# Attention with a mixture of experts on one core: the transition's masks, first gathers, first expert products and last gate weights in another order

## Chip, cores and metric

One Trainium2 chip, 1 core. The metric is the device time of one execution, in microseconds (us).

## What is computed

8 batches of 8 heads of causal attention (576 positions, head size 64, a bias from a running sum, softmax) give 4608 rows of 512 numbers. Each row goes to one of 16 experts and comes back times its gate weight:

```python
scores = scale * np.matmul(q, k.transpose(0, 1, 3, 2))
scores = np.where(causal, -1000000000.0, scores + np.minimum(bias, 0.0))
attn = np.exp(scores - np.max(scores, axis=-1, keepdims=True))
attn_out = np.matmul(attn / (np.sum(attn, axis=-1, keepdims=True) + 1e-09), v)
x = attn_out.transpose(0, 2, 1, 3).reshape(B * S, H * D)
g_idx = np.argmax(x @ w_group, axis=1)            # 4 groups
# within a group: e_idx = argmax(x @ w_expert[g]), 4 experts each
h = np.maximum(x[mine] @ w1[g, e], 0.0)           # 512 -> 1024
out[mine] = (g_w * e_w)[mine][:, None] * (h @ w2[g, e])
```

## The kernel before

**Attention and routing.** The heads run through a pipeline: row maxima (PE, DVE), scores (PE), exp from PSUM into the tiles pt and pu (ACT, L274), zeros above the diagonal by an affine select on POOL (`mask`, L283), then the product with the values (PE, L304), copied out by ACT. Pairs of heads are normalised and transposed into xT (DVE), rounded to xTh (ACT, L362) with the remainder xTl (L366), and turned back into rows that a DMA stores to the DRAM tensor xs. `Router.batch` follows a batch behind: logits, their transposes plt (L789), a chain on DVE from the maximum to the one-hot `hot` (L797 to L818), counts per expert by PE products into pc (L825), then on DVE the place of each row (L842 to L858), its selector tiles col, rows and val (L862 to L873), and products `listed` (L880) that write the row numbers (pi) and the gate weights (pw) of each expert's list. The weights come from Exp (L897) and a chain of twelve small operations (L904 to L922), which ACT writes back as c3p (L923); val 2 to 4 (L931) wait for it, and pw for them.

**Experts.** Each of 16 slots takes one expert's rows by indirect DMA from xs (`gather`, L599, on POOL's queue), transposes them on PE (px, L1058), splits each into a rounded part (xh, ACT, L1059) and the remainder (xl, DVE, L1060), and multiplies: eight groups ph (L1108) with the rounded weights wh and both parts, then with the low weights wl and xh; a group's relu is split again into hh (ACT, L1103) and hl (DVE, L1104); then four groups py of w2 (L1163). Rounded weights are cast by ACT (L1007), the low ones made by POOL (L1010) or DVE (L1016). The first slot takes 256 rows of an expert that is chosen behind batch 6, so that it can start before the last batch is routed; `start()` does that: it reduces the lists to ids, issues two gathers and picks the next expert. The last batch's rows of that expert make one more tile of 128, `rest` (its transposed rows prr, split in xhr and xlr, L1237 to L1240; products pur, L1250). Slot 1 has 368 rows.

**What sets the order.** PE's order in the transition is that of the program text, inside `manual_schedule(engines={ENG.PE})` (L1337 on), where `run` calls lists of items one by one. The orders of DVE, ACT and POOL there come from a scheduler of the framework. `after(tc, i)` holds back what is issued until i is issued; `behind(tc, later, earlier)` orders two instructions of one engine without a semaphore. A key chain on DVE (L1305 to L1317: key, rank, sel, esl, esi) ranks the experts for the later slots.

Of the kernel before, what the change touches and what calls it, by code (L numbers as in the profile page):

```python
# [8 lines left out]
F32 = mybir.dt.float32  # L9
# [45 lines left out]
def attn_moe(ctx, tc, qk, v, s, wr, w1, w2, out, stop_at=None, dbg=None):  # L55
# [24 lines left out]
    st.listed = {}  # L80

# [29 lines left out]
def attention(tc, qk, v, s, wr, xs, st):  # L111
# [3 lines left out]
    with ExitStack() as ctx:  # L115
# [138 lines left out]
        def scores(n, pt):  # L254
# [23 lines left out]
            def causal(u):  # L278
# [4 lines left out]
                nc.gpsimd.affine_select(out=d, in_=d, pattern=[[0, len(u)], [1, rows]], compare_op=ALU.is_ge, fill=0.0,  # L283
                                        base=0, channel_multiplier=-1)
# [3 lines left out]
        def av(n, pt, vals, sums):  # L288
# [4 lines left out]
            for half, todo in enumerate(avs):  # L293
# [4 lines left out]
                def item(j, t, qa, qb, half=half, base=base, w=w, po=po, last=len(todo) - 1):  # L298
                    if j == 0:
# [4 lines left out]
                    nc.tensor.matmul(po[0][:, qa - base:qb - base],  # L304
                                     VT[p % NVT].rearrange("p t a d -> p (t a d)")[:, (3 * t + 1 + h) * 64:][:, 0:P],
                                     x[:, c:c + qb - qa], start=(j == 0), stop=(j == last))
                    if j == last:
# [13 lines left out]
        def normalise(p, vals, sums):  # L321
# [312 lines left out]
class Router:  # L634
# [106 lines left out]
    def start(self):  # L741
# [3 lines left out]
        first_ids(nc, sm, st, 0, 2, ((0, 0, 2, st.ids0[:, 0:2]),))  # L745
        for t in range(2):
            st.gathered = gather(nc, self.xs, st.xg0, P, t, st.ids0[:, t:t + 1], NTOK - S)
        yield
        self.pick(1)
        t = sm.tile([P, E], F32, name="ku")  # L750
        V.tensor_scalar(out=t, in0=st.count, scalar1=-1.0, scalar2=256.0, op0=ALU.mult, op1=ALU.add)
        V.scalar_tensor_tensor(out=t, in0=t, scalar=0.0, in1=st.first[:, 0], op0=ALU.max, op1=ALU.mult)
        V.tensor_tensor(out=st.count, in0=st.count, in1=t, op=ALU.add)
        yield

    def batch(self, b, xtail, xh, xl):
# [857 lines left out]
```

## Time and profile before

| | |
|---|---|
| median of 3 runs | 928.27 us (927.01 to 928.57) |
| the profiled execution's own time | 927.77 us |
| its span, first to last instruction | 926.1 us |
| mean granted clock of TensorE | 0.987 |
| busy: PE, DVE, ACT, POOL | 93, 76, 68, 71% |

Attention takes up about 0 to 445 us of the span, the experts about 445 to 912. A busy share is an average over both. A wait is idle time of an engine with the instruction that released it; the granted clock is a share of full speed, in a stretch or over the whole.

### The profile page before, as it was taken

What the parts mean: (1) busy time and instruction counts of PE and PEld (TensorE: products, weight loads), DVE (VectorE), ACT (ScalarE), POOL (GpSimd) and SP (SyncE); (2) the same over time, 40 slices, a digit from 0 to 9 for tenths busy, and PEclk for the clock granted to TensorE, in tenths of its full rate; (3) what the DMA queues carried; (4) which work ended last, traced back from release to release, by engine and by line L of the source; (5) the groups of instructions that cost most, each with busy time, mean ns of one, the idle gap of its engine ahead of it and who ended that gap; (6) DMA issues with size and microseconds to landing.
All of it is one profiled execution on the core that took longest, in us unless ns stands there. A gap on an engine that the chain in (4) does not pass through costs nothing. (4 is left out here: it accounts for less than half of the span.)

```text
span 926.1 us, 17738 instructions
## 1 busy us (share of the span) xinstructions
PE 864.9 (93%) x5649; PEld 780.6 (84%) x5649; DVE 701.4 (76%) x1989; ACT 629.5 (68%) x1373; POOL 660.1 (71%) x762
## 2 busy tenths in 40 slices
PE   4899999999999999998879999999999999999993
PEld 3788787888878787887778999899999999999992
DVE  7676686858778686866476788899888889888830
ACT  3688787888878787876736666666676666776640
POOL 8798686877868686844678656666678778877750
PEclk9999999999999999999989999999999999999997
DMA  7766655565646665323537545446555555665510
GB/s 150 182 165 164 147 143 145 144 157 140 155 107 159 147 156 134 101 84 138 188 128 225 182 173 184 166 163 218 193 203 183 192 185 207 229 218 194 181 44 23
DMA packets 65005, 148.10 MB, mean 160 GB/s; under 512 B 7588, under 2 KB 40996, under 8 KB 54728
## 3 DMA queue, kind: packets, MB, share of 16 engines
q1 hardware_dynamic: 55020, 126.98, 46.6%
q0 software_dynamic: 7488, 18.89, 5.7%
q10 hardware_dynamic: 2396, 1.02, 0.4%
q8 instruction: 47, 0.77, 0.4%
q14 instruction: 54, 0.44, 0.2%
HBM read 108.97 MB, written 19.69 MB: 139 GB/s over the span
## 5 line engine op out<-in xcount | busy, mean ns | idle before, releaser
L1010 POOL TENSOR_TENSOR wl<-raw,wh 128x512 fp32r<-128x512 f32 x182 | 232.9, 1302 | 59.7 <-ACT wh L1007 41.7
L158 POOL TENSOR_TENSOR WB<-r,WA 64x576 fp32r<-64x576 f32 x128 | 181.3, 1416 | 23.5 <-PE pm L207 10.9
L215 DVE CUSTOM_DVE_ANT_0 mx<-pm,mask 128x192 bf16<-128x192 f32 (+4 forms) x320 | 129.1, 419 | 39.1 <-PE pm L207 34.4
L1007 ACT CAST wh<-raw 128x512 fp32r<-128x512 f32 x256 | 153.9, 616 | 1.0 <-POOL wl L1010 0.7
L1108 PE MATMUL ph<-xl,wh 128*128 128x256 f32 (+13 forms) x512 | 146.8, 306 | 4.5 <-DVE xl L1080 4.5
L1108 PE MATMUL ph<-xh,wh 128*128 128x256 f32 (+13 forms) x512 | 145.5, 302 | 3.9 <-DVE xl L1060 2.7
L264 PE MATMUL ps<-WA 68*128 68x320 f32 (+4 forms) x384 | 136.6, 359 | 6.8 <-ACT pu L274 3.6
L207 PE MATMUL pm<-WA 66*128 66x288 f32 (+4 forms) x384 | 124.9, 353 | 17.4 <-DMA WA<-ch 9.8
L304 PE MATMUL po<-pt,VT 128*128 128x256 f32 (+3 forms) x512 | 122.1, 355 | 2.5 <-POOL pt L283 2.5
L1163 PE MATMUL py<-hl,wh 128*128 128x256 f32 (+13 forms) x448 | 113.4, 302 | 1.3 <-DVE hl L1104 1.3
L1163 PE MATMUL py<-hh,wh 128*128 128x256 f32 (+13 forms) x448 | 112.8, 301 | 0.0
L266 PE MATMUL ps<-WB 128*128 128x320 f32 (+4 forms) x384 | 110.6, 301 | 0.0
L1209 DVE STREAM_TRANSPOSE yr<-yT 32x384 f32<-32x384 f32 (+1 forms) x208 | 104.5, 502 | 4.3
L304 PE MATMUL po<-pu,VT 128*128 128x320 f32 (+1 forms) x384 | 105.2, 381 | 0.0
L1075 DVE STREAM_TRANSPOSE xt<-xg 32x256 f32<-32x256 f32 (+1 forms) x208 | 102.5, 493 | 3.2
L1108 PEld LDWEIGHTS ph<-xl,wh 128*128 128x128 f32 x512 | 97.8, 191 | 7.9 <-DVE xl L1080 6.4
L1108 PEld LDWEIGHTS ph<-xh,wh 128*128 128x128 f32 x512 | 97.8, 191 | 5.9 <-DVE xl L1060 3.0
L304 PEld LDWEIGHTS po<-pt,VT 128*128 128x128 f32 x512 | 87.4, 192 | 14.7 <-POOL pt L283 3.0
L1103 ACT ACTIVATE hh<-ph 128x256 fp32r<-128x256 f32 (+13 forms) x128 | 53.5, 420 | 62.3 <-PE ph L1108 61.9
L207 PEld LDWEIGHTS pm<-WA 66*128 66x128 f32 (+1 forms) x384 | 68.5, 190 | 30.6 <-DVE mc L215 13.1
L283 POOL TENSOR_SCALAR_AFFINE_SELECT pt<-pt 128x128 f32<-128x128 f32 (+2 forms) x192 | 63.7, 341 | 42.0 <-ACT pt L274 37.1
L1104 DVE SCALAR_TENSOR_TENSOR hl<-ph,hh 128x256 fp32r<-128x256 f32 (+13 forms) x128 | 59.3, 464 | 41.1 <-ACT hh L1103 39.2
(225 smaller groups left out, 1948.8 us busy)
## 6 DMA issues: line engine op xcount, KB each, us to landing
raw<-in_w_dram SPq DMA_DIRECT2D x64, 1024.0 KB
WB<-WA SPq DMA_DIRECT2D x64, 288.0 KB
r<-in_qk_dram SPq DMA_DIRECT2D x31, 576.0 KB
VT<-in_v_dram SPq DMA_DIRECT2D x32, 384.0 KB
xs<-xr SPq DMA_DIRECT2D x15, 512.0 KB
xs<-xrt SPq DMA_DIRECT2D x7, 128.0 KB
xg<-xs,ids POOLq DMA_INDIRECT x46, 4.5
out_dram<-yr,ids POOLq DMA_INDIRECT x43, 3.2
```

The lines of the kernel that those rows point to most:

```text
L158: i = nc.gpsimd.tensor_tensor(out=wb[64 * a:64 * a + 64, a, h], in0=r[:, h, a], in1=w[0:64, a, h, QO:].bitcast(F32), op=ALU.subtract)
L207: nc.tensor.matmul(ps[:rows, :cw], WA[i][0:66, QA, h, QO + q0:QO + q0 + rows], WA[i][0:66, KA, h, QO + c0:QO + c0 + cw], start=True, stop= ...
L215: nc.vector.tensor_tensor_reduce(out=tmp[:rows, :cw], in0=ps[:rows, :cw], in1=mk[:rows], scale=1.0, scalar=-3.0e38 if c0 == 0 else mo, op0 ...
L264: nc.tensor.matmul(ps[:rows, o:o + w], WA[i][0:68, KA, h, QO + k0:QO + k0 + rows], WA[i][0:68, QA, h, QO + q0:QO + q0 + w], start=True, st ...
L266: nc.tensor.matmul(ps[:rows, o:o + w], WB[p % NBB][:, KA, h, k0:k0 + rows], WB[p % NBB][:, QA, h, q0:q0 + w], start=False, stop=True)
L304: nc.tensor.matmul(po[0][:, qa - base:qb - base], VT[p % NVT].rearrange("p t a d -> p (t a d)")[:, (3 * t + 1 + h) * 64:][:, 0:P], x[:, c: ...
L1007: self.casts.append(nc.scalar.copy(h[:, j], raw[:, j]))
L1010: self.low = nc.gpsimd.tensor_tensor(out=l[:, j], in0=raw[:, j], in1=h[:, j].bitcast(F32), op=ALU.subtract)
L1075: V.transpose(dst[:, 0:n, :, j], src[:, 0:n, :, i])
L1108: self.product = nc.tensor.matmul(pss[f][:, :cap], w[f // 4][:, c, (f % 4) * P:(f % 4 + 1) * P], x[:, c, :cap], start=(c == 0 and w is sel ...
L1163: self.product = nc.tensor.matmul(pss[c][:, :cap], w[2 + f // 4][:, f % 4, c * P:(c + 1) * P], x[:, f, :cap], start=(f == 0 and w is self. ...
L1209: V.transpose(dst[:, 0:n, :, i], src[:, 0:n, :, j])
```

## The change

Four things, and the bookkeeping for them (lists st.masks, st.av, st.lows, st.counted, st.valued and products, to which instructions are appended as they are issued):

- `start()` yields twice more before the gathers and once between them; the second gather is ordered behind the third mask from the end, and a low part of xT (st.lows[-3]) behind the last mask. The choice of the next expert comes after the ids are written.
- The first slot's groups 0 to 3 are opened together on column blocks 0 and 1, then on 2 and 3; the transposes of its gathered rows are ordered ahead of the fourth attention product from the end; the first weight cast is ordered behind the xh of the last transposes, as `split` then names it, and the third behind the last sums of attention. The last batch's counts stand ahead of product 84 (the low products of group 5).
- `weights()` is the old code from Exp to c3p as a function. For the last batch it runs ahead of pi, with a PSUM tile of its own (pk) in place of room in pi's, and is no longer held behind the first ids.
- pi stands behind 40 products of py, pw behind all the first 24 low ones; the key chain comes after val 4, not after the first ids.

```diff
@@ -742,15 +745,18 @@
 
         nc, sm, st = self.tc.nc, self.sm, self.st
         V = nc.vector
-        first_ids(nc, sm, st, 0, 2, ((0, 0, 2, st.ids0[:, 0:2]),))
+        chosen = first_ids(nc, sm, st, 0, 2, ((0, 0, 2, st.ids0[:, 0:2]),))
+        yield
+        yield
         for t in range(2):
-            st.gathered = gather(nc, self.xs, st.xg0, P, t, st.ids0[:, t:t + 1], NTOK - S)
-        yield
-        self.pick(1)
-        t = sm.tile([P, E], F32, name="ku")
-        V.tensor_scalar(out=t, in0=st.count, scalar1=-1.0, scalar2=256.0, op0=ALU.mult, op1=ALU.add)
-        V.scalar_tensor_tensor(out=t, in0=t, scalar=0.0, in1=st.first[:, 0], op0=ALU.max, op1=ALU.mult)
-        V.tensor_tensor(out=st.count, in0=st.count, in1=t, op=ALU.add)
+            st.gathered.append(gather(nc, self.xs, st.xg0, P, t, st.ids0[:, t:t + 1], NTOK - S))
+            yield
+        with after(self.tc, chosen):
+            self.pick(1)
+            t = sm.tile([P, E], F32, name="ku")
+            V.tensor_scalar(out=t, in0=st.count, scalar1=-1.0, scalar2=256.0, op0=ALU.mult, op1=ALU.add)
+            V.scalar_tensor_tensor(out=t, in0=t, scalar=0.0, in1=st.first[:, 0], op0=ALU.max, op1=ALU.mult)
+            V.tensor_tensor(out=st.count, in0=st.count, in1=t, op=ALU.add)
         yield
 
     def batch(self, b, xtail, xh, xl):
...
@@ -886,41 +892,44 @@
                 V.tensor_tensor(out=dst, in0=dst, in1=ps[:, 0:(j1 - j0) * EL], op=ALU.add)
             return ps
 
-        yield 2
-        pi = listed(0, 2, "pi")
-        if b == B - 1:
-            st.routed = first_ids(nc, sm, st, 0, 3, ((0, 2, 3, st.ids0[:, 2:3]), (1, 0, 3, st.ids1)))
-        if b == B - 2:
-            for _ in self.start():
-                yield
-
-        nc.scalar.activation(ex, df, AF.Exp)
-        yield 1
-        wf = pi[:, 128:128 + NB * 5]
-        w = wf.rearrange("p (t g) -> p t g", g=5)
-        cwp, rem = pi[:, 160:160 + NB], pi[:, 168:168 + NB]
-        c3p = pi[:, 176:176 + 3 * NB].rearrange("p (j t) -> p j t", t=NB)
-        with after(tc, st.routed):
+        def weights(bank):
+            nc.scalar.activation(ex, df, AF.Exp)
+            yield 1
+            wf = bank[:, 128:128 + NB * 5]
+            w = wf.rearrange("p (t g) -> p t g", g=5)
+            cwp, rem = bank[:, 160:160 + NB], bank[:, 168:168 + NB]
+            c3p = bank[:, 176:176 + 3 * NB].rearrange("p (j t) -> p j t", t=NB)
             V.tensor_reduce(out=wf, in_=ex, axis=AX.X, op=ALU.add)
             V.tensor_scalar(out=wf, in0=wf, scalar1=1e-9, scalar2=None, op0=ALU.add)
             V.reciprocal(wf, wf)
-        yield
-        with after(tc, st.routed):
+            yield
             ws = T("ws", [NB, 4])
             V.tensor_tensor(out=ws, in0=w[:, :, 1:5], in1=oh[:, :, 0], op=ALU.mult)
             wsum = T("wsum", [NB])
             V.tensor_reduce(out=wsum, in_=ws, axis=AX.X, op=ALU.add)
             for x in (cwp, st.cw[:, b]):
                 V.tensor_tensor(out=x, in0=wsum, in1=w[:, :, 0], op=ALU.mult)
-        yield
-        with after(tc, st.routed):
+            yield
 
             c3 = T("c3", [3, NB], BF16)
             V.tensor_copy(c3[:, 0], cwp)
             V.tensor_tensor(out=rem, in0=cwp, in1=c3[:, 0], op=ALU.subtract)
             V.tensor_copy(c3[:, 1], rem)
             V.tensor_tensor(out=c3[:, 2], in0=rem, in1=c3[:, 1], op=ALU.subtract)
-        nc.scalar.copy(c3p, c3)
+            nc.scalar.copy(c3p, c3)
+            return c3, c3p
+
+        yield 2
+        if b == B - 1:
+            c3, c3p = yield from weights(self.ps_s(f"pk{b}"))
+        pi = listed(0, 2, "pi")
+        if b == B - 1:
+            st.routed = first_ids(nc, sm, st, 0, 3, ((0, 2, 3, st.ids0[:, 2:3]), (1, 0, 3, st.ids1)))
+        else:
+            if b == B - 2:
+                for _ in self.start():
+                    yield
+            c3, c3p = yield from weights(pi)
         for j in range(3):
             yield
             with after(tc, st.routed):
...
@@ -928,7 +937,8 @@
                     nc.gpsimd.tensor_tensor(out=val[:, 2 + j], in0=colf, in1=c3[:, j].unsqueeze(2).to_broadcast(C4),
                                             op=ALU.mult)
                 else:
-                    V.tensor_tensor(out=val[:, 2 + j], in0=colf, in1=c3p[:, j].unsqueeze(2).to_broadcast(C4), op=ALU.mult)
+                    st.valued = V.tensor_tensor(out=val[:, 2 + j], in0=colf,
+                                                in1=c3p[:, j].unsqueeze(2).to_broadcast(C4), op=ALU.mult)
         yield 2
         if b == B - 2:
             yield
...
@@ -1092,9 +1104,20 @@
                 def first(f):
 
                     pss[f] = acc(f"ph{u}_{f}")
-                    for c in range(4):
+                    half(f, 0)
+                    half(f, 2)
+
+                def half(f, c0):
+                    for c in (c0, c0 + 1):
                         for x in (self.xh, self.xl):
                             product(f, self.w.h, x, c)
+
+                def opening():
+                    for f in range(4):
+                        pss[f] = acc(f"ph{u}_{f}")
+                    for c in (0, 2):
+                        for f in (0, 3, 1, 2):
+                            half(f, c)
 
                 def last(f):
                     for c in range(4):
...
@@ -1114,8 +1137,8 @@
 
                 if u == 0:
 
-                    return [lambda f=f, part=part: part(f) for h in (0, 4) for part in (first, last)
-                            for f in range(h, h + 4)]
+                    return [opening] + [lambda f=f, part=part: part(f) for part, h in ((last, 0), (first, 4), (last, 4))
+                                        for f in range(h, h + 4)]
                 return [lambda f=f: item(f) for f in range(8)]
 
             def y_rows(self):
...
@@ -1285,7 +1308,10 @@
         cws = mc.tile([P, E, NL], F32, name="cws")
         wts = [Expert(0, st.e0[0:1, 0:1]), Expert(1, st.e0[0:1, 1:2])]
         first = Slot(0, wts[0], 256, xgs[0], st.ids0[:, 0:2], cws[:, 0])
-        first.last = st.gathered
+        first.last = st.gathered[1]
+        for i, k in ((1, 3),):
+            behind(tc, st.gathered[i], st.masks[-k])
+        behind(tc, st.lows[-3], st.masks[-1])
         rest = Tile("r", wts[0], xgs[0], st.ids0[:, 2:3], cws[:, 0, 2:3])
         run(wts[0].load((st.evacs[-3], st.xh, st.xrt, st.xrt), (first.last,) * 4, nc.gpsimd))
         rest.gather()
...
@@ -1296,7 +1322,7 @@
         with after(tc, slots[1].last, rest.last):
             nc.gpsimd.memset(yT[:, :, 2 * P:], 0.0)
 
-        order = after(tc, st.routed)
+        order = after(tc, st.valued)
 
         S3 = [P, E, E]
         ie, key, t3 = st.ie, st.key, st.t3
...
@@ -1336,15 +1362,20 @@
 
         with tc.manual_schedule(engines={ENG.PE}):
             run(X)
+            behind(tc, st.av[-4], first.turned)
+            behind(tc, wts[0].casts[0], first.split[0])
+            behind(tc, wts[0].casts[2], st.evacs[-1])
             h = first.h_items()
-            run(h[:12])
-            behind(tc, st.listed[0], first.product)
-            run(h[12:])
+            run(h)
+            made = first.products
+            behind(tc, made[84], st.counted)
             Y, R = first.y_items(), rest.items()
-            run(Y[:4])
-
-            behind(tc, st.listed[2], first.product)
-            run(Y[4:6] + R[:1])
+            del made[:]
+            run(Y[:6])
+            behind(tc, st.listed[0], made[39])
+            behind(tc, made[40], st.listed[0])
+            behind(tc, st.listed[2], made[-1])
+            run(Y[6:7] + R[:1])
             with after(tc, rest.split[1]):
                 by_slot(idf, idl, 0, E)
                 listed = V.tensor_copy(ids, idf)
...
@@ -1354,7 +1385,7 @@
                 V.tensor_tensor(out=cwl, in0=part[3], in1=part[4], op=ALU.add)
                 V.tensor_tensor(out=cwl, in0=cwl, in1=part[2], op=ALU.add)
                 by_slot(cws, cwl, 0, 1)
-            run(Y[6:] + R[1:5])
+            run(Y[7:] + R[1:5])
             W = wts[1].load((first.rounded, rest.split[0], None, None), (None, rest.split[1], None, None))
             run(W[:8])
             low = wts[1].low
```

On **POOL**, at the end of attention (pt and pu are the tiles of exp, two of each for two heads; xg the gathered rows). Before:

```order
L283 AFFINE_SELECT pu_118<-pu_118 128x128
L283 AFFINE_SELECT pt_117<-pt_117 64x64
L599 DMA xg_74<-xs,ids_69 128x512 x2
L283 AFFINE_SELECT pt_117<-pt_117 128x2x128
L928 TENSOR_TENSOR val_6109<-col_6093,c_6209 128x320
L283 AFFINE_SELECT pt_119<-pt_119 64x64
L283 AFFINE_SELECT pt_119<-pt_119 128x128
L283 AFFINE_SELECT pu_120<-pu_120 128x128
L283 AFFINE_SELECT pt_119<-pt_119 128x2x128
L366 TENSOR_TENSOR xTl_6036<-xT_6180,xTh_6035 128x512
```

With the change:

```order
L284 AFFINE_SELECT pu_118<-pu_118 128x128
L284 AFFINE_SELECT pt_117<-pt_117 128x2x128
L284 AFFINE_SELECT pt_117<-pt_117 64x64
L602 DMA xg_74<-xs,ids_69 128x512
L284 AFFINE_SELECT pt_119<-pt_119 64x64
L284 AFFINE_SELECT pt_119<-pt_119 128x128
L602 DMA xg_74<-xs,ids_69 128x512
L937 TENSOR_TENSOR val_6109<-col_6093,c_6228 128x320
L284 AFFINE_SELECT pu_120<-pu_120 128x128
L284 AFFINE_SELECT pt_119<-pt_119 128x2x128
L369 TENSOR_TENSOR xTl_6036<-xT_6162,xTh_6035 128x512
```

Both masks of the first head have moved in front of the first gather, two of the second head's between the gathers, and val behind both gathers.

On **DVE**, from the last batch's one-hot and counts to the lists (hl the remainder of a group of the first slot). Before:

```order
L818 TENSOR_TENSOR hot<-oh_6347,plt_6333 128x80
L1104 SCALAR_TENSOR_TENSOR hl_6593<-ph_4_6654,hh_6592 128x256
L842 TENSOR_TENSOR pc_6351<-pc_6351,count 128x80
L1104 SCALAR_TENSOR_TENSOR hl_6593<-ph_5_6663,hh_6592 128x256
L1104 SCALAR_TENSOR_TENSOR hl_6593<-ph_6_6672,hh_6592 128x256
L844 TENSOR_TENSOR off_6364<-pc_6351,hot 128x80
L845 TENSOR_TENSOR count<-count,pc_6351 128x16
L1104 SCALAR_TENSOR_TENSOR hl_6593<-ph_7_6681,hh_6592 128x256
L849 TENSOR_REDUCE pos<-off_6364 128x5
L849 TENSOR_REDUCE pc_6351<-off_6364 128x5
L854 TENSOR_TENSOR u_6369<-pc_6351,thr 128x20
L856 TENSOR_REDUCE pc_6351<-u_6369 128x5
```

With the change, a piece from the middle of the same stretch, behind the place chain that is interleaved with the gate weights:

```order
L915 CAST c_6392<-pk_6381 128x5
L868 TENSOR_TENSOR col_6374<-hot,pc_6351 128x320
L873 TENSOR_TENSOR rows_6376<-cols,pc_6351 128x640
L916 TENSOR_TENSOR pk_6381<-pk_6381,c_6392 128x5
L1127 SCALAR_TENSOR_TENSOR hl_6594<-ph_5_6664,hh_6593 128x256
L1127 SCALAR_TENSOR_TENSOR hl_6594<-ph_6_6673,hh_6593 128x256
L879 TENSOR_TENSOR val_6378<-col_6374,part 128x320 x2
L1127 SCALAR_TENSOR_TENSOR hl_6594<-ph_7_6682,hh_6593 128x256
L917 CAST c_6392<-pk_6381 128x5
L918 TENSOR_TENSOR c_6392<-pk_6381,c_6392 128x5
L892 TENSOR_TENSOR lists<-lists,pi_6398 128x128
```

hl of groups 5 to 7 stood right behind pc; now 5 and 6 stand behind rows, 7 behind val, and the gate weights' chain (c, pk) ends in front of the lists.

On **DVE**, around the second lists (xts and idl are made from the lists for all slots, wl is a weight of slot 1). Before:

```order
L1315 TENSOR_REDUCE esl<-t_73 128x16
L922 TENSOR_TENSOR c_6411<-pi_6381,c_6411 128x5
L1317 CAST esi<-esl 128x16
L931 TENSOR_TENSOR val_6378<-col_6374,pi_6381 128x320 x3
L886 TENSOR_TENSOR lists<-lists,pw_6420 128x192
L615 TENSOR_SCALAR xts<-idl 128x64
L616 SCALAR_TENSOR_TENSOR idl<-idl,xts 128x64
L1016 TENSOR_TENSOR wl_0_6874<-raw_0_6872,pw_0_0_6886 128x512
L1240 TENSOR_TENSOR xlr<-prr_x,xhr 128x4x128
L1329 TENSOR_TENSOR xts<-sel,idl 128x1024
L1016 TENSOR_TENSOR wl_1_6877<-raw_1_6875,pw_1_0_6897 128x512
```

With the change:

```order
L1337 TENSOR_TENSOR sel<-rank,ie 128x256
L892 TENSOR_TENSOR lists<-lists,pw_6421 128x192
L618 TENSOR_SCALAR xts<-idl 128x64
L1340 TENSOR_TENSOR t_73<-sel,ie 128x256
L619 SCALAR_TENSOR_TENSOR idl<-idl,xts 128x64
L1341 TENSOR_REDUCE esl<-t_73 128x16
L1343 CAST esi<-esl 128x16
L1026 TENSOR_TENSOR wl_0_6875<-raw_0_6873,pw_0_0_6887 128x512
L1263 TENSOR_TENSOR xlr<-prr_x,xhr 128x4x128
L1355 TENSOR_TENSOR xts<-sel,idl 128x1024
L1026 TENSOR_TENSOR wl_1_6878<-raw_1_6876,pw_1_0_6898 128x512
```

The val rows have left this place, and t, esl and esi of the key chain now stand between the lists and xlr.

## Rows read from the trace of the kernel before

**Rows 1.** The page, busy time by engine: us, share of the span, instructions.

```profile
...
PE 864.9 (93%) x5649; PEld 780.6 (84%) x5649; DVE 701.4 (76%) x1989; ACT 629.5 (68%) x1373; POOL 660.1 (71%) x762
```

**Rows 2.** Waits of PE, 425 to 500 us: line that waited, what released it, us in total, times, longest.

```profile
...
PE pw L880 <- DVE val L931: 5.1, 1, 5.1
PE ph L1108 <- DVE xl L1060: 2.7, 1, 2.7
PE po L304 <- POOL pt L283: 2.1, 1, 2.1
```

**Rows 3.** The same, 500 to 926 us.

```profile
...
PE ph L1108 <- DVE xl L1080: 4.5, 9, 1.0
```

**Rows 4.** Stretches of 2 us: length, PE busy (instructions), granted clock, DMA share, GB/s.

```profile
...
434.00:436.00 2.00, 1.30 (x3) 0.67 0.70 215
436.00:438.00 2.00, 2.00 (x9) 0.50 0.05 21
...
480.00:482.00 2.00, 1.11 (x6) 0.50 0.67 178
482.00:484.00 2.00, 2.00 (x10) 0.50 0.11 41
484.00:486.00 2.00, 2.00 (x12) 0.53 0.00 0
```

**Rows 5.** Timeline of PE: start, us, line, operation, out<-in, count [idle before <-releaser].

```profile
...
434.70 1.43 PE L304 MATMUL po<-pt,VT 128*128 128x320 f32 x2 [2.08 <-POOL pt L283]
...
439.48 0.27 PE L1058 MATMUL px<-ident,xg 128*128 128x128 f32 x1
...
447.61 0.39 PE L1108 MATMUL ph<-xh,wh 128*128 128x256 f32 x1 [2.73 <-DVE xl L1060]
...
453.03 0.76 PE L1108 MATMUL ph<-xh,wl 128*128 128x256 f32 x5
...
462.82 2.08 PE L1108 MATMUL ph<-xh,wl 128*128 128x256 f32 x16
464.74 0.32 PE L825 MATMUL pc<-hot,ub 128*128 128x64 bf16 x2
...
472.94 0.56 PE L880 MATMUL pi<-val,rows 128*128 128x128 bf16 x5
...
480.89 1.09 PE L880 MATMUL pw<-val,rows 128*128 128x192 bf16 x5 [5.05 <-DVE val L931]
```

**Rows 6.** Timeline of POOL, the same columns.

```profile
...
431.65 1.26 POOL L599 DMA_INDIRECT xg<-xs,ids  x1 [0.94 <-DVE c L919]
433.21 1.00 POOL L599 DMA_INDIRECT xg<-xs,ids  x1 [0.31 <-issue]
434.23 0.41 POOL L283 TENSOR_SCALAR_AFFINE_SELECT pt<-pt 128x256 f32<-128x256 f32 x1
...
480.46 0.54 POOL L1297 MEMSET yT<- 128x512 f32 x1
480.95 3.75 POOL L1010 TENSOR_TENSOR wl<-raw,wh 128x512 fp32r<-128x512 f32 x3
485.28 4.78 POOL L1010 TENSOR_TENSOR wl<-raw,wh 128x512 fp32r<-128x512 f32 x3 [0.58 <-ACT wh L1007]
```

**Rows 7.** Timeline of ACT.

```profile
...
428.52 0.60 ACT L274 ACTIVATE pt<-ps 128x512 f32<-128x512 f32 x1
...
479.35 0.17 ACT L923 CAST pi<-c 128x15 f32<-128x15 bf16 x1 [14.03 <-DVE c L922]
```

**Rows 8.** DMA issues, 430 to 440 us: count, KB each, median us from issue to landing.

```profile
...
xg<-xs,ids POOLq DMA_INDIRECT x2, 3.7
```

**Rows 9.** Timeline of DVE, from the last batch's logits to the end of its gate weights.

```profile
...
460.92 0.26 DVE L797 TENSOR_REDUCE lmx<-plt 128x25 f32<-128x100 f32 x1 [1.36 <-PE plt L789]
...
462.80 0.24 DVE L818 TENSOR_TENSOR hot<-oh,plt 128x80 bf16<-128x80 f32 x1
...
465.50 0.25 DVE L842 TENSOR_TENSOR pc<-pc,count 128x80 f32<-128x80 f32 x1 [0.59 <-PE pc L825]
...
466.55 0.42 DVE L1104 SCALAR_TENSOR_TENSOR hl<-ph,hh 128x256 fp32r<-128x256 f32 x1
...
468.55 0.81 DVE L867 TENSOR_TENSOR rows<-cols,pc 128x640 bf16<-128x640 f32 x1
469.28 1.65 DVE L873 TENSOR_TENSOR val<-col,part 128x320 bf16<-128x320 bf16 x2
...
475.63 0.26 DVE L904 TENSOR_REDUCE pi<-df 128x25 f32<-128x100 f32 x1
...
479.22 0.17 DVE L1317 CAST esi<-esl 128x16 int32<-128x16 f32 x1
```

**Rows 10.** Timeline of DVE, the lists and what follows.

```profile
...
474.13 0.19 DVE L615 TENSOR_SCALAR kemp<-kids 128x48 f32<-128x48 f32 x1
...
482.02 0.35 DVE L886 TENSOR_TENSOR lists<-lists,pw 128x192 f32<-128x192 f32 x1 [1.19 <-PE pw L880]
482.30 2.47 DVE L615 TENSOR_SCALAR xts<-idl 128x64 f32<-128x64 f32 x1
...
485.58 0.68 DVE L1240 TENSOR_TENSOR xlr<-prr_x,xhr 128x512 fp32r<-128x512 f32 x1
486.18 1.48 DVE L1329 TENSOR_TENSOR xts<-sel,idl 128x1024 f32<-128x1024 bf16 x1
```

More of the change, by code (lines that the diff above doesn't have):

```diff
@@ L80, in attn_moe @@
     st.listed = {}
+    st.masks, st.av, st.gathered, st.lows = [], [], [], []
     attention(tc, qk, v, s, wr, xs, st)
@@ L282, in causal @@
                 d = probs(pt, t, off)[:rows, 0:len(u) * w].rearrange("p (t q) -> p t q", q=w)[:, :, 0:rows]
-                nc.gpsimd.affine_select(out=d, in_=d, pattern=[[0, len(u)], [1, rows]], compare_op=ALU.is_ge, fill=0.0,
-                                        base=0, channel_multiplier=-1)
+                st.masks.append(nc.gpsimd.affine_select(out=d, in_=d, pattern=[[0, len(u)], [1, rows]],
+                                                        compare_op=ALU.is_ge, fill=0.0, base=0, channel_multiplier=-1))
             return [lambda u=u: item(u) for u in units]
@@ L303, in item @@
                             (pt[0], PC[t]))
-                    nc.tensor.matmul(po[0][:, qa - base:qb - base],
+                    i = nc.tensor.matmul(po[0][:, qa - base:qb - base],
                                      VT[p % NVT].rearrange("p t a d -> p (t a d)")[:, (3 * t + 1 + h) * 64:][:, 0:P],
                                      x[:, c:c + qb - qa], start=(j == 0), stop=(j == last))
+                    if n == NH - 1 and half:
+                        st.av.append(i)
                     if j == last:
@@ L824, in count @@
         def count(lhs, t0, t1, col, rows=P, start=False, stop=False):
-            nc.tensor.matmul(pc[:, col:col + (t1 - t0) * E], lhs[:rows],
-                             ohb[:rows, t0:t1].rearrange("p t e -> p (t e)"), start=start, stop=stop)
+            st.counted = nc.tensor.matmul(
+                             pc[:, col:col + (t1 - t0) * E], lhs[:rows], ohb[:rows, t0:t1].rearrange("p t e -> p (t e)"), start=start, stop=stop)
         count(self.ub, 0, 4, 0, start=True)
@@ L1043, in __init__ @@
                 self.rows = [min(P, cap - t) for t in range(0, cap, P)]
+                self.products = []
             def gather(self):
@@ L1107, in product @@
                 def product(f, w, x, c):
-                    self.product = nc.tensor.matmul(pss[f][:, :cap], w[f // 4][:, c, (f % 4) * P:(f % 4 + 1) * P], x[:, c, :cap],
-                                     start=(c == 0 and w is self.w.h and x is self.xh), stop=(c == 3 and w is self.w.l))
+                    self.products.append(nc.tensor.matmul(pss[f][:, :cap], w[f // 4][:, c, (f % 4) * P:(f % 4 + 1) * P], x[:, c, :cap],
+                                     start=(c == 0 and w is self.w.h and x is self.xh), stop=(c == 3 and w is self.w.l)))
                 def item(f):
@@ L1162, in product @@
                 def product(c, w, x, f, stop=None):
-                    self.product = nc.tensor.matmul(pss[c][:, :cap], w[2 + f // 4][:, f % 4, c * P:(c + 1) * P], x[:, f, :cap],
+                    self.products.append(nc.tensor.matmul(pss[c][:, :cap], w[2 + f // 4][:, f % 4, c * P:(c + 1) * P], x[:, f, :cap],
                                      start=(f == 0 and w is self.w.h and x is self.hh),
-                                     stop=(f == 7 and w is self.w.l) if stop is None else stop)
+                                     stop=(f == 7 and w is self.w.l) if stop is None else stop))
                 def item(c):
```

7 lines of the change are left out of this document (4 added, 3 removed).

## Prediction

> **What bounds the kernel now.** I read the page first, then the table of waits of TensorE for the transition and for what follows, then granted clock and busy time in short stretches, then the timelines of the four engines around each wait. The page says that PE is busy for 93% of the span [rows 1]: only time in which PE stands, or runs at its lower level, can be won. The transition from attention to the experts (about 425 to 500 us) holds 9.9 us of waits in three places: an attention product that waits for the causal mask (2.1), the first expert product that waits for the split of its gathered rows (2.7), and the last list product that waits for the gate weights (5.1) [rows 2]. In the 426 us behind it the largest sum of waits is 4.5 us for xl, in nine pieces [rows 3], so that what the transition gains should arrive at the end. The reader is to see in the stretches that each long wait has a second cost: behind the first and the last the granted clock is 0.50 to 0.67 while PE is fully busy, the lower of the two levels, 1.2 and not 2.4 GHz [rows 4]. In PE's timeline the same shows behind the second: 32 products take 5.42 us (447.61 to 453.03), whereas 16 with the same columns take 1.92 (462.82 to 464.74), 0.12 each [rows 5]. All is summed against the profiled execution, 927.77 us, 0.50 below the median of the runs shown.
>
> **What the change removes.**
>
> 1. *The mask.* Its input is ready at 429.12 (428.52 + 0.60) [rows 7], but POOL holds two gathers in front of it and masks at 434.23 [rows 6]. Now both masks of that head stand before the first gather. The wait goes, 2.08 [rows 5], and the half clock behind it: 1.30 us busy and 2.00 us busy, all at half, lose 0.65 + 1.00 = 1.65 [rows 4]. Removed: 3.73.
>
> 2. *The opening.* Four groups use the first two column blocks before the last two, so xl of blocks 2 and 3 is needed 16 products (1.9 us) later; besides, the transposes for these blocks stand ahead of the last attention products. The wait of 2.73 goes, and 5.42 − 32 × 0.12 = 1.6 of half clock [rows 5]. The low weights that POOL makes take 4 × 1.25 us (3.75 for 3 in [rows 6]); the fourth hangs on a later cast, but the 32 products, 3.84 us, cover it. Removed: 4.33.
>
> 3. *The gate weights.* Exp to c3 runs beside the counts, so the cast that waited 14.03 us for c [rows 7] comes before pi. The wait of 5.05 goes [rows 5], and behind it 1.11 × 0.50 + 2.00 × 0.50 + 2.00 × 0.47 = 2.5 us of half clock [rows 4]. Removed: 7.55.
>
> Together 3.73 + 4.33 + 7.55 = 15.6 us.
>
> **What it adds.**
>
> 4. *The second gather* now starts behind two more small masks, near 433.75 instead of 433.21 [rows 6]; it lands 3.7 later [rows 8], 437.45. PE came to the first transpose at 439.48; without item 1's 3.73, and with an attention product and a half now in front, it is at the second near 436.6 [rows 5]. Wait: 0.85. The list product of batch 6 stands there too and needs val, which POOL now makes behind that gather: between 0 and 1.2, I take 0.4. Who waits behind is xh, xl and the opening, all with time to spare.
>
> 5. *The counts* are forced ahead of the fifth group's end. Between the transposes of the logits and the counts PE has 11 products left, 1.32 us; DVE's chain from the first reduction (460.92) to hot (462.80 + 0.24) takes 2.12 [rows 9], with a tenth on either side. Wait: 0.9. Before, 32 products covered it.
>
> 6. *hl behind the router.* DVE now runs ten small gate-weight operations and the router's chain in front of hl of groups 5 and 6, and both val in front of hl of group 7. Before, hl of 5 to 7 followed the pc row at once and was done by 466.97, that is 1.47 behind pc's start (465.50) [rows 9]. Now pc to rows takes 465.50 to 469.36, 3.86, less the 1.1 of the three hl (0.42 for one alone), plus 1.4 for the gate weights, ten at 0.14 (475.63 to 479.22 holds 21, wider ones among them, 0.17 each): hl 5 is there 4.2 behind pc, hl 6 at 4.55, hl 7 at 6.4, behind val's 1.65 [rows 9]. PE needs hl 5 after 12 + 11 products, 2.76, and hl 7 four later. Wait: 1.6 + 1.6 = 3.2. Two such waits in a row are nearest to the 2.08 one, so I add its half clock, 1.65 (between 0 and that).
>
> 7. *The rows of the `rest` tile (xlr).* With the weights' wait gone, PE comes to xlr's first use sooner: 24 products, 24 low ones, the five of pw, four transposes and eight more behind pi, about 8.1 us behind pi's end. DVE's path to xlr is lists, xts, idl, wl, xlr: 482.02 to 486.26 [rows 10], 4.24, of which the xts row takes 2.47 although the same form took 0.19 at 474.13. Without that hold it is 1.94; to it come three operations of the key chain that now stand in between, 1.0. Lists can start 6.5 behind pi's end, so xlr is there at 9.4, a wait of 1.35. With one hold as in the row, 2.3 more and the half clock of item 1 as well: 1.35 + 2.3 + 1.65 = 5.3. I take that, because POOL's wl run stands beside these operations as before, and now starts 7.0 behind pi (the memset at 480.46 [rows 6] against the end of pi at 473.5 [rows 5]). The bounds are 1.35 and 10.9 (second rival).
>
> The row shows the small operation start at 482.30, stand through the boundary between two POOL operations, and end 0.07 us behind the run (480.95 + 3.75 = 484.70); yet the 1024-wide one at 486.18, beside the next run, took 1.48 for sixteen times the elements [rows 10]. So the hold is neither certain nor limited to one POOL operation. The Trainium skill ("SBUF — State Buffer", section "SBUF: two separate sides") says that GpSimd and VectorE share a pair of ports, locked for one whole instruction by whoever starts first. By it three operations would wait at most one wl each, 3 × 1.25 = 3.75 in place of 2.3, and the time would be 925.9 instead of 924.5; the 2.47 row speaks against a hold that short, no row for three in a row.
>
> The key chain itself, the moved pi and Exp, and SP's queue cost nothing: pi's val is ready before PE comes, since some 25 of the 40 products ahead of pi come behind the hl waits, and no DMA of SP is moved.
>
> **The sum.** Removed 15.6; added 0.85 + 0.4 + 0.9 + 3.2 + 1.65 + 5.3 = 12.3. Net 3.3: 927.77 − 3.3 = **924.5 us**.
>
> **Rivals.**
>
> *No hold on DVE.* xlr waits 1.35 only: 15.6 less items 4 to 6, 7.0, less 1.35 is 7.25, time 920.5; without half clock behind the hl waits, 918.9. For it: the gathers, not wl, run while the first of these DVE operations go; the 1024-wide row. Against: the 2.47 row.
>
> *The hold lasts the whole run (slower).* One mechanism at item 7: DVE's small operations get in only when POOL pauses. Before, a pause came after three wl, because POOL waited 0.58 for ACT [rows 6]. Now ACT's casts no longer stand behind the late c3 cast, and POOL goes on: gathers to 7.0, two wl, the memset (0.54), four wl, to 15.0 behind pi's end. Then xlr is there at 17.3, a wait of 9.2, with half clock 10.9: 15.6 − 7.0 − 10.9 = −2.3, time 930.1. It decides from the point where DVE misses the first boundary, and costs more than all that item 3 brings.
>
> *The gain doesn't stay.* The waits change places: the hl and gather waits come out larger, or the experts, entered sooner, wait for weights (POOL's wl, 1.25 each, is next in line). Something of 6 to 7 us lost elsewhere gives 927 to 928. For it: items 4 to 7 are five new waits in 50 us. Against: they are short by the rows, and PE stood hardly at all in the experts' stage [rows 3]. That the change does not do what it says is part of this case: in the order on POOL and DVE masks and weights do move, so only the two lines on the casts are left that move nothing visible.
>
> **How the numbers follow.** Forecast 45%, no hold 24%, whole-run hold 14%, gain lost 17%. What a measurement can tell from no change is 0.2%, 1.9 us. Faster: the first two less a little, 0.68; same: the last with that little, 0.18; slower: 0.14. The range goes from just under the no-hold case, 918.5, to the whole-run case, 930.3; beyond either end there is under one chance in ten. The likeliest case alone holds 922 to 926.
>
> **What would show it.** In the waits of the changed kernel: no wait of po for the mask, none of the first ph for xl, none of pw for val; instead px on the gather (0.85), pc on hot (0.9), py on hl (3.2 in two pieces), pur on xlr (1.4 to 4). Clock at 1.00 where rows 4 show half, except behind py's wait. On DVE, whether an operation between lists and xlr takes over 1 us decides between forecast and first rival; if it takes over 5, the slow rival holds. I am wrong if the half clock comes back with waits this short, which I can't exclude, or if the experts' stage takes longer than before.

## The result, and the profile after

| | before | changed |
|---|---|---|
| median of the runs shown together | 927.75 us (4 runs) | 934.63 us (933.13 to 936.64, 4 runs) |
| the profiled execution's own time | 927.77 us | 936.64 us |
| its span | 926.1 us | 934.9 us |
| mean granted clock | 0.987 | 0.982 |

The ratio is 1.0075, 95% interval 1.0052 to 1.0098: the change makes the kernel **slower by 0.75%**, and lies above the range that was given. The three long waits did go; another of 8.65 us came.

First the waits of PE, 425 to 500 us of the changed kernel (us in total, times, longest), against [rows 2]:

```profile
...
PE pur L1273 <- DVE xlr L1263: 8.6, 1, 8.6
PE py L1186 <- DVE hl L1127: 3.6, 2, 2.5
PE pw L886 <- DVE val L940: 1.3, 1, 1.3
PE pc L831 <- DVE hot L824: 1.2, 2, 0.7
PE px L1069 <- DMA xg<-xs,ids: 0.6, 1, 0.6
```

None of the three lines of [rows 2] is left as it was: po no longer waits for the mask, ph no longer for xl, and pw only 1.3 (it is batch 6's pw, not the last batch's). Their place was taken by pur, which waits 8.6 for xlr.

PE's timeline in the transition, against [rows 5]:

```profile
...
435.38 0.70 PE L305 MATMUL po<-pt,VT 128*128 128x320 f32 x2
...
441.80 0.69 PE L886 MATMUL pw<-val,rows 128*128 128x192 bf16 x5 [1.26 <-DVE val L940]
...
447.58 0.36 PE L1131 MATMUL ph<-xh,wh 128*128 128x256 f32 x1
...
451.49 2.08 PE L1131 MATMUL ph<-xh,wl 128*128 128x256 f32 x16
...
467.47 0.38 PE L1186 MATMUL py<-hl,wh 128*128 128x256 f32 x1 [1.14 <-DVE hl L1127]
...
470.81 0.58 PE L1186 MATMUL py<-hl,wh 128*128 128x256 f32 x1 [2.50 <-DVE hl L1127]
...
483.79 0.50 PE L1273 MATMUL pur<-wh,xhr 128*128 128x512 f32 x1
492.94 0.80 PE L1273 MATMUL pur<-wh,xlr 128*128 128x512 f32 x1 [8.65 <-DVE xlr L1263]
```

The reader should see four things. The product at 434.70 in [rows 5], minus its wait of 2.08, would have started at 432.62; the same one is at 435.38 here without a wait, so that 2.8 us were lost ahead of the transition. The opening takes 447.58 to 451.49: its 32 products take 3.91, not 5.42. The two waits for hl are there, 1.14 and 2.50. And between the first and the second product of pur stand 8.65 us.

What was lost ahead of the transition is a matter of the clock. The stretches (length, PE busy, granted clock, DMA share, GB/s):

```profile
...
150.00:200.00 50.00, 48.12 (x295) 0.97 0.54 132
200.00:250.00 50.00, 48.35 (x299) 0.97 0.56 140
```

PE's order of work there is that of the kernel before, it is busy as always in attention, and yet the clock is 0.97 twice, which costs 100 × 0.03 = 3.0 us. The profile of the kernel before shows 1.00 in both stretches. So does another execution with the same code there (e1 below), which has 0.97 from 300 to 400 us instead. Runs of one kernel lie some us apart for such reasons, which no run explains. I therefore put down 2.8 of the spans' difference of 8.8 us to chance and **6.0 to the change**. Behind 500 us PE's waits are the same small ones, xl 4.5 in nine pieces as in [rows 3], so that the transition holds all of the 6.0.

The stretches of 2 us around the waits that are left, against [rows 4]:

```profile
...
442.00:444.00 2.00, 2.00 (x12) 0.75 0.00 0
444.00:446.00 2.00, 2.00 (x10) 0.50 0.12 40
446.00:448.00 2.00, 2.00 (x11) 0.90 0.70 230
470.00:472.00 2.00, 1.19 (x5) 0.57 0.16 66
472.00:474.00 2.00, 2.00 (x13) 0.57 0.66 164
492.00:494.00 2.00, 1.06 (x3) 0.50 0.48 66
494.00:496.00 2.00, 2.00 (x6) 0.50 0.85 360
496.00:498.00 2.00, 2.00 (x7) 0.60 1.01 422
```

Half clock stands behind the wait of batch 6's pw, behind the second wait for hl, and behind pur's.

Where xlr was, DVE's timeline tells, against [rows 9, 10]:

```profile
...
467.00 0.75 DVE L1127 SCALAR_TENSOR_TENSOR hl<-ph,hh 128x256 fp32r<-128x256 f32 x2
467.67 2.75 DVE L879 TENSOR_TENSOR val<-col,part 128x320 bf16<-128x320 bf16 x2
...
482.51 8.07 DVE L618 TENSOR_SCALAR xts<-idl 128x64 f32<-128x64 f32 x1
490.50 0.41 DVE L1340 TENSOR_TENSOR t<-sel,ie 128x256 f32<-128x256 bf16 x1
...
492.20 0.68 DVE L1263 TENSOR_TENSOR xlr<-prr_x,xhr 128x512 fp32r<-128x512 f32 x1
```

The 64-wide xts takes 8.07 us; the same form on 48 columns took 0.19 [rows 10]. Nothing that follows up to 497 us takes over 1.3 us. POOL at the same time, against [rows 6]:

```profile
...
482.67 2.52 POOL L1020 TENSOR_TENSOR wl<-raw,wh 128x512 fp32r<-128x512 f32 x2
485.12 0.52 POOL L1323 MEMSET yT<- 128x512 f32 x1
485.61 4.92 POOL L1020 TENSOR_TENSOR wl<-raw,wh 128x512 fp32r<-128x512 f32 x4
```

Two wl, the memset and four wl run back to back from 482.67 to 490.53; xts ends at 490.58. In the kernel before the run was cut at 484.70, since POOL waited for a cast, and xts ended at 484.77 [rows 6, 10]. The cast for which it waited then comes at the same time in both kernels (ACT, before and changed):

```profile
...
484.59 1.66 ACT L1007 CAST wh<-raw 128x512 fp32r<-128x512 f32 x3
```

```profile
...
484.67 1.66 ACT L1017 CAST wh<-raw 128x512 fp32r<-128x512 f32 x3
```

What moved is POOL: its first wl starts at 482.67 and not at 480.95, and the memset (0.5) stands between the second and the third. So it comes to the fourth wl 2.1 us later, when the cast is done.

### The profile page after: what moved, and what is told of

Same layout as the page of the kernel before. It is cut to its first block, busy times and chain, and to the rows that moved or that the text cites. A ratio compares the mean times of both kernels' runs of the same rounds, so it can differ in the third digit from the quotient of the medians.

```text
span 934.9 us, 17742 instructions
## 1 busy us (share of the span) xinstructions
PE 868.4 (93%) x5649; PEld 781.9 (84%) x5649; DVE 707.3 (76%) x1989; ACT 629.3 (67%) x1373; POOL 659.3 (71%) x762
## 5 line engine op out<-in xcount | busy, mean ns | idle before, releaser
L305 PE MATMUL po<-pu,VT 128*128 128x320 f32 (+1 forms) x384 | 107.7, 389 | 0.0
L1131 PE MATMUL ph<-xh,wl 128*128 128x256 f32 (+13 forms) x512 | 90.0, 299 | 0.0
```

What stands on the lines that cost most here:

```text
L305: i = nc.tensor.matmul(po[0][:, qa - base:qb - base], VT[p % NVT].rearrange("p t a d -> p (t a d)")[:, (3 * t + 1 + h) * 64:][:, 0:P], x[: ...
L1131: self.products.append(nc.tensor.matmul(pss[f][:, :cap], w[f // 4][:, c, (f % 4) * P:(f % 4 + 1) * P], x[:, c, :cap], start=(c == 0 and w ...
```

## Experiments

The median of the kernel before was 926.7 to 927.3 beside each of them; what counts is the difference within a group.

**e1: xts out of the way.** With a scratch tile of its own the scheduler places xts early on DVE, beside the gathers:

```diff
-        list_ids(nc, st, idl, t4[:, 0], 0, NL)
+        emp = mc.tile(S3L, F32, name="emp")
+        list_ids(nc, st, idl, emp, 0, NL)
```

> The changed kernel, but the operation xts (the 64-wide tensor_scalar in front of idl) writes to a scratch tile of its own, so that DVE runs it and idl beside the gathers, ahead of the lists of pw; nothing else moves. Theory A (this one operation is held through POOL's whole run of wl: 8.07 us in the changed kernel, 0.2 without): the wait of pur for xlr falls from 8.65 to under 1.5, the half clock behind it (2.1) mostly goes, time 925 to 927.5 against 934.6. Rival B (any DVE operation there is held, or PE simply comes too early for xlr): the next operation, t or wl, takes 5 us or more, the wait stays above 6, time 932 to 935.

Measured: 933.86 us, 1.0062 (1.0042 to 1.0082); the wait for xlr 8.5. DVE's timeline, and POOL's:

```profile
...
482.94 8.30 DVE L1340 TENSOR_TENSOR t<-sel,ie 128x256 f32<-128x256 bf16 x1
```

```profile
...
483.10 2.52 POOL L1020 TENSOR_TENSOR wl<-raw,wh 128x512 fp32r<-128x512 f32 x2
485.56 0.52 POOL L1323 MEMSET yT<- 128x512 f32 x1
486.04 4.92 POOL L1020 TENSOR_TENSOR wl<-raw,wh 128x512 fp32r<-128x512 f32 x4
```

Theory A falls. xts is out of the way, and the next operation, t, takes 8.30, until the run of POOL (483.10 to 490.96) is over.

**e2: another form at the same place**, for this one call (`oob` is a constant tile):

```diff
...
+    else:
+        V.scalar_tensor_tensor(out=emp, in0=ids, scalar=0.0, in1=oob, op0=ALU.is_equal, op1=ALU.mult)
...
-        list_ids(nc, st, idl, t4[:, 0], 0, NL)
+        list_ids(nc, st, idl, t4[:, 0], 0, NL, st.oob)
```

> The changed kernel with xts at its place, but in another form: scalar_tensor_tensor with a constant tile as second input, instead of tensor_scalar with one input. Theory A1 (the form decides: an operation with two SBUF inputs gets in at the next boundary between two POOL operations, the one-input form doesn't): xts takes at most 1.3 us, xlr waits 1 to 3, time 925.5 to 929. Theory A2 (every operation from SBUF to SBUF is held until POOL pauses): xts takes about 8 us again, time 933 to 936.

Measured: 934.23 us, 1.0073 (1.0048 to 1.0098). DVE's timeline:

```profile
...
480.23 8.09 DVE L623 SCALAR_TENSOR_TENSOR xts<-idl,oob 128x64 f32<-128x64 f32 x1
```

One input or two makes no difference: A1 falls, A2 holds.

**e4: hl ahead of the router's tiles** (with e1's edit; `place` is the instruction that makes col, `left` the one of hl of group 7):

```diff
+            behind(tc, st.place, first.left)
```

> As e1_own_scratch, and DVE runs hl of groups 5 to 7 ahead of col, rows and val of the last batch. Theory (the two waits of py for hl, 3.6 together, and the half clock behind them, 1.4, come from DVE's order): both waits under 0.5 in sum, 3.5 to 5 us faster than e1_own_scratch, 921 to 923. Rival (the wait moves: val comes later, and pi waits for it instead): pi waits 2 us or more, time within 1.5 of e1_own_scratch.

Measured: 929.03 us, 1.0020 (1.0003 to 1.0037), 4.8 less than e1 on the same chip. Waits of PE:

```profile
...
PE pur L1273 <- DVE xlr L1263: 8.6, 1, 8.6
...
```

py waits for hl no more, and pi does not wait for val. That part of the loss was DVE's order, and its size as expected; the absolute time was not (921 to 923), since e1 had not gained.

**e5: masks, gathers and opening alone.** The gate weights, pi, pw and the key chain as before, and the counts are no longer forced ahead of product 84:

```diff
-            behind(tc, made[84], st.counted)
...
-            behind(tc, st.listed[0], made[39])
-            behind(tc, made[40], st.listed[0])
-            behind(tc, st.listed[2], made[-1])
...
+            behind(tc, st.listed[0], first.products[60])
+            behind(tc, first.products[61], st.listed[0])
...
+            behind(tc, st.listed[2], first.products[79])
...
```

> The masks and gathers and the opening of four groups alone; the last batch's gate weights, pi, pw and the key chain stand as in the kernel before (pi behind 61 products of py, pw behind 16 low ones). Theory from the trace of the changed kernel (masks and gathers net nothing, 3.7 removed and 3.6 added by the gather's, pw's and half clock's share; the opening brings 4.3, of which counts and hl behind the router take 1.2 + 2 to 4 back): 925.5 to 928.5, no measurable difference to before, pw still waiting about 5 for val. Rival (the forecast's items 1, 2, 4 and 5 hold, and only the gate weights' move is bad): 8.1 removed, 2.2 added, 921 to 923.

Measured: 930.18 us, 1.0038 (1.0017 to 1.0059): slower than either expectation. Waits of PE:

```profile
...
PE py L1183 <- DVE hl L1124: 4.8, 3, 2.6
...
```

py waits more for hl, 4.8 in three pieces, with no gate weights beside the counts at all, and pw still waits 6.1 for val. So the gate weights are not needed to push hl back. DVE's scheduler puts the router's chain (col, rows, val) in front of hl as soon as the opening and its orders are there; in e8, without them, it doesn't, and there is no such wait. Why it does is open: around the counts PE's order is the same in e5 and e8.

**e6: POOL pauses.** A one-element addition on POOL reads what DVE writes last, and the six wl of slot 1 stand behind it:

```diff
+            paused = nc.gpsimd.tensor_tensor(out=pause, in0=cws[:, 0, 0:1], in1=cws[:, 0, 0:1], op=ALU.add)
...
+            for i in wts[1].lows:
+                behind(tc, i, paused)
```

> The changed kernel with a pause on POOL: a one-element addition that reads DVE's cws stands in front of the six wl of slot 1, so POOL starts them only when DVE has finished the chain from the lists to cws. e1_own_scratch showed that the operation is not the point (with xts out of the way, t took 8.30). Theory C (the first DVE operation whose operands all lie in SBUF and that meets POOL's run is held until that run ends): with POOL idle none of DVE's operations there takes over 1.3 us, xlr's wait falls from 8.6 to under 1.5, half clock behind it goes too, time 924 to 926.5 against 934.6. Rival D (the loss returns elsewhere: the six wl come 6 us later, and the low products of slot 1 wait for them): a wait of ph for wl of 3 us or more, time 928 to 932. Rival E (DVE is slow there for another reason): t or xts still takes 5 us or more, 933 to 936.

Measured: 927.68 us, 1.0002 (0.9985 to 1.0018), the profiled execution 925.96. DVE's timeline, and POOL's:

```profile
...
479.63 0.19 DVE L618 TENSOR_SCALAR xts<-idl 128x64 f32<-128x64 f32 x1
479.74 0.42 DVE L1342 TENSOR_TENSOR t<-sel,ie 128x256 f32<-128x256 bf16 x1
...
```

```profile
...
486.30 0.19 POOL L1390 TENSOR_TENSOR pause<-cws 128x1 f32<-128x1 f32 x1 [7.26 <-DVE cws L1359]
486.44 8.42 POOL L1020 TENSOR_TENSOR wl<-raw,wh 128x512 fp32r<-128x512 f32 x6
```

Waits of PE:

```profile
...
PE pur L1274 <- DVE xlr L1264: 0.8, 1, 0.8
...
```

Up to xlr DVE's order is that of the changed kernel, and no operation takes over 1.3 us: xts 0.19 where it took 8.07, and t 0.42 where it took 8.30 in e1. This is **theory C**: the hold comes from POOL's run. The time lies between the ranges of C (924 to 926.5) and D (928 to 932). Of 10.9 us (8.65 of wait and 2.3 of half clock) 6.4 are won by the medians, each against its own runs of before; most of the rest went to a wait of pur for ACT's xhr (1.3), 0.8 for xlr and 1.1 for hl of slot 1. No product waits for wl, so rival D isn't seen.

**e7: both repairs**, e4's edits and the pause:

```diff
+        emp = mc.tile(S3L, F32, name="emp")
+        list_ids(nc, st, idl, emp, 0, NL)
...
+            behind(tc, st.place, first.left)
...
+            for i in wts[1].lows:
+                behind(tc, i, paused)
```

> Both repairs together: e4_hl_first (xts early, hl of groups 5 to 7 ahead of col, rows, val; 929.0) and the pause on POOL. By theory C the 8.6 us wait and 2.1 of half clock go from 929.0: 918.5 to 921.5, faster than the kernel before (926.7) by 0.6 to 0.9%. By rival D, 923 to 927.

Measured: 921.87 us (919.93 to 924.53), 0.9939 (0.9917 to 0.9961): **faster than the kernel before by 0.6%**, 5.8 less than e6 on the same chip, and 0.4 above the upper end of theory C's range. Waits of PE, 425 to 510 us:

```profile
...
PE pur L1274 <- ACT xhr L1263: 1.4, 1, 1.4
...
PE ph L1132 <- DVE hl L1128: 1.1, 1, 1.1
...
PE pur L1274 <- DVE xlr L1264: 0.6, 1, 0.6
```

**e8: masks and gathers alone**, on the kernel before: `start()` as in the change and:

```diff
-        first.last = st.gathered
+        first.last = st.gathered[1]
+        behind(tc, st.gathered[1], st.masks[-3])
+        behind(tc, st.lows[-3], st.masks[-1])
```

> The kernel before with the masks and gathers (start) of the change alone. From the trace of the changed kernel this part removes 2.1 of wait and 1.65 of half clock and adds 0.6 (px on the gather), 1.2 (pw of batch 6 on val, because one xT operation on DVE is held beside POOL's xTl) and 1.7 of half clock: net nothing, 926 to 928. By the forecast's items 1 and 4: 3.73 removed, 1.25 added, 923.5 to 925. If it is slower than 929, the loss of e5_front_parts sits here and not in the opening.

Measured: 924.88 us, 0.9971 (0.9958 to 0.9984). Waits of PE:

```profile
...
PE ph L1112 <- DVE xl L1064: 1.6, 1, 1.6
```

It brings 2.3 by the medians, not nothing: the forecast's items 1 and 4 (3.73 less 1.25) were nearer than my reading of the changed trace. po waits no more, and the first ph waits 1.6 for xl where it waited 2.7; that second part stands in neither sum, so the agreement is in part luck.

**e9: order instead of a pause** (on e4):

```diff
-        V.tensor_copy(esi, esl)
+        behind(tc, st.added, V.tensor_copy(esi, esl))
...
+            behind(tc, listed, slots[1].split[1])
```

> As e4_hl_first (929.0), with two more orders on DVE and no pause on POOL: t, esl and esi stand ahead of the lists of pw, in the gap in which DVE waited 0.9 for pw, and the cast of the ids with what follows stands behind the four xl of slot 1. So no operation whose operands all lie in SBUF is left between the lists and xlr; wl and xlr read PSUM. Theory C (such operations are held through POOL's run, those that read PSUM are not): xlr is there in time, its wait falls from 8.6 to under 1.5, 919 to 922 if the 1024-wide xts that follows gets in at a boundary between two wl, as it did before (1.48), and 923 to 927 if it is held to the run's end, since xl of slot 1 stands behind it. Rival (whatever DVE does beside POOL's run is held, PSUM or not): wl or xlr takes 5 us or more, 928 to 931.

Measured: 929.10 us, 1.0011 (0.9994 to 1.0028), a miss. DVE's timeline, and POOL's:

```profile
...
477.92 4.65 DVE L1343 CAST esi<-esl 128x16 int32<-128x16 f32 x1
482.49 0.34 DVE L892 TENSOR_TENSOR lists<-lists,pw 128x192 f32<-128x192 f32 x1
```

```profile
...
478.35 2.50 POOL L1020 TENSOR_TENSOR wl<-raw,wh 128x512 fp32r<-128x512 f32 x2
480.79 0.52 POOL L1323 MEMSET yT<- 128x512 f32 x1
481.27 1.25 POOL L1020 TENSOR_TENSOR wl<-raw,wh 128x512 fp32r<-128x512 f32 x1
485.60 3.95 POOL L1020 TENSOR_TENSOR wl<-raw,wh 128x512 fp32r<-128x512 f32 x3 [3.07 <-ACT wh L1017]
```

t and esl now ran in time, but esi, 16 wide, began 0.4 before POOL's run and was held 4.65 us, until POOL stopped to wait for a cast (481.27 + 1.25 = 482.52). Everything behind it on DVE, the lists of pw first, came over 4 later, and pur waited 4.7 for xhr. DVE's wl and xlr, which read PSUM, were not held, but had no wl of POOL beside them, so that the rival isn't decided by this run.

**e10: the front parts with hl first** (on e5):

```diff
+            behind(tc, st.place, first.left)
```

> As e5_front_parts (930.2: masks, gathers and the opening; gate weights as before), with hl of groups 5 to 7 ahead of col, rows and val on DVE. It tells what the opening is worth beside e8_masks_gathers (924.9). Theory (the opening's loss of 5 is the three waits for hl, 4.8, and the half clock behind them): no wait for hl, 921 to 924, so that the opening then gains 1 to 4. Rival (PE only comes to pw sooner, whose val hangs on DVE's chain and not on PE): the wait of pw grows to 7 or more, 924 to 927, and the opening is worth nothing by itself.

Measured: 922.84 us, 0.9966 (0.9948 to 0.9983). Waits of PE:

```profile
...
PE py L1183 <- DVE hl L1124: 1.0, 1, 1.0
...
```

Of the three waits for hl one is left, 1.0, in front of py's first product. Against e8 the opening brings 2.0 by the medians but 0.5 by the ratios, whose intervals overlap, so that a gain from it is not shown. Against e5 the order of hl brings 7.9 by the medians, each against its own runs of before.

## Why the prediction was wrong

**Items 1 to 3, what is removed: the waits right, the clock only in part.** 2.08, 2.73 and 5.05 went, and the opening's 1.6 of half clock. But half clock came back elsewhere: 1.7 behind the wait of batch 6's pw (stretches 442 to 448: 0.5 + 1.0 + 0.2), 1.4 behind hl and 2.3 behind pur. That is 5.4 for the 5.75 that the forecast removed, and the text had named it as what could prove it wrong. How much returns is in part chance: e4 and e9 have such stretches behind batch 6's pw too, but e1, e2, e6, e7 and e8, with the same wait there (1.1 to 1.3), show 1.00 throughout 434 to 448.

**Items 4 to 6, the new waits: right within 0.9 each.** px on the gather 0.58 for 0.85, batch 6's pw 1.26 for 0.4 (its upper end was 1.2), pc on hot 0.72 for 0.9, py on hl 3.64 for 3.2, with 1.4 of half clock for 1.65. Two of the causes given were not right. For hl, the router's chain in front of it was; the ten gate-weight operations were not needed, since e5 has the waits without them. And pw waited for the val of DVE, not of POOL: DVE's xT in front of it took 1.83 beside POOL's xTl (438.98 to 440.25), where the one before it took 0.76 (435.22):

```profile
...
439.03 1.83 DVE L352 TENSOR_TENSOR xT<-vals,st 128x576 f32<-128x576 f32 x1
```

**Item 7 is the step that failed.** I took one hold "as in the row, 2.3 more". It was 7.9 more (8.07 − 0.19), the wait 8.65 and not 3.65, and 2.3 of half clock stood behind it (stretches 492 to 498: 0.53 + 1.0 + 0.8). That is the mechanism of the slow rival, to which I gave 14%. It put POOL's run at 7.0 to 15.0 behind pi's end, and the run stood at 7.0 to 14.8. That its 10.9 meets the measured 8.65 + 2.3 = 10.95 to the tenth is luck: its wait, 9.2, was too long and its half clock, 1.65, too short. Its reason was not quite right either, since the cast that had cut the run came no earlier. The row had told of the hold: xts of [rows 10] stood through a boundary and ended 0.07 behind the end of POOL's run. What it stood through was the *rest of that run*, 2.4 us, and the order of the change showed a run of about 8 in the same place; I carried the old length over. e6 shows it by taking the run away, with DVE's order up to xlr untouched. By the rule that I weighed (the Trainium skill, "SBUF — State Buffer", section "SBUF: two separate sides": the pair of ports is locked for one whole instruction), as I read it, an operation would wait for at most one wl, 1.25. The trace shows it waiting through seven instructions, and the trace decides.

**Why above the rival's 930.1.** Rival: 2.3 slower, net. On top of it come 1.7 of half clock from item 1 and 0.6 more in item 4; that gives 4.6 of the 6.0 us. The remaining 1.4 I can't assign. It does not lie in waits: between the same two points of its work PE stood 10.2 us before (424.9 to 505.0: 80.1 long, 69.9 busy) and 15.2 in the changed kernel (427.8 to 513.8: 86.0 and 70.8), which the waits in the tables account for, and was busy 0.9 longer. The 2.8 us that the profiled execution lost ahead of the transition I count as no part of the change; the median, 6.9 above before, has less of it.

**Even without the hold the sum was too good.** e6's profiled execution took 925.96, where the rival without a hold said 920.5. Item 7 explains why the change came out slower, but not the whole distance to the forecast.

**The sum by experiments.** 6.9 over before; the pause takes away 6.4 to 7.6 (the change to e6, e4 to e7, each against its own runs of before), hl's order 4.8 to 5.8 (e1 to e4, e6 to e7). With both taken away (e7) the change is worth −5.3: 2.3 for masks and gathers (e8), 0.5 to 2 for the opening (e8 to e10), and 0.9 by the medians or 2.5 by the ratios for the gate weights' move with its pause (e10 to e7), which the forecast had down for 7.55. As I read it, DVE's chain behind pw is short of cover, and most of the 5.05 comes back in smaller waits (xhr 1.35, xlr 0.65, hl of slot 1 1.1 in e7); no run tests that by itself.

Not settled: why some operations get in between two instructions of POOL and others don't, why DVE's scheduler moves hl with the opening, the last 1.4 us, and what sets the extra stretches of lower clock within attention.

## What to carry to other kernels

An operation that is slow once beside another engine's run is priced by that run's length in the *new* order, not by what it lost in the old one; look where its end falls, and if that is the end of the neighbour's run, it is a hold and not a cost of its own. A pause of a neighbour can be useful: in the kernel before POOL stood 0.58 for a cast, and in that pause DVE worked. The change did not move the cast; it started POOL's run later and put a memset inside it, so that POOL no longer had to wait. Ask of every pause that an operation relies on whether both of its sides stay where they are. When a wait of PE is removed, read the next chain on the engine that fed it before booking the gain; here more than all of it came back.

## What the runs showed of the hardware

Some operations of DVE whose operands all lie in SBUF, and which met a run of tensor_tensor (and a memset) on POOL, were held to the end of the run. These six were, in four forms and of several widths:

| kernel | operation on DVE | took | its end | POOL's run ended |
|---|---|---|---|---|
| before | xts, tensor_scalar, 64 wide | 2.47 | 484.77 | 484.70 |
| changed | the same | 8.07 | 490.58 | 490.53 |
| e1 | t, tensor_tensor, 256 wide | 8.30 | 491.24 | 490.96 |
| e2 | xts, scalar_tensor_tensor, 64 wide | 8.09 | 488.32 | 488.23 |
| e4 | t, tensor_tensor, 256 wide | 8.31 | 486.15 | 485.87 |
| e9 | esi, cast, 16 wide | 4.65 | 482.57 | 482.52 |

In e5, e8 and e10 the same xts again took 2.45 to 2.46 and ended 0.06 to 0.07 behind the end of a run of three wl. The rows show what ended a hold, not what began it: in the five later lines of the table the operation began 0.13 to 0.43 ahead of POOL's first wl, beside the end of a gather, and esi, 0.17 long elsewhere [rows 9], would have been over before it.

It is not always so. Of the changed kernel, the two val of 320 bf16 elements (467.67, 2.75 for both) ran while POOL was in a run that lasted from 461.13 to 471.55, and the 1024-wide xts of [rows 10] took 1.48 beside another. A reduction between SBUF tiles was not held at all beside that run of 10.4 us:

```profile
...
464.39 0.23 DVE L855 TENSOR_REDUCE pos<-off 128x5 f32<-128x80 f32 x1
```

hl and xlr, which read PSUM, took their usual 0.4 to 0.7 beside POOL's runs in the rows shown (hl at 467.00, xlr of [rows 10] at 485.58).
